# First batch of an attention-and-FFN kernel: one load, two fillers, one quad's division and its banks moved

## The chip, the cores and the metric

The kernel runs on one core of a Trainium2 chip. The core has a matrix engine (TensorE, in the profile PE, its weight loads PEld), a vector engine (VectorE, DVE), an activation engine (ScalarE, ACT), GpSimd (POOL) and a sync engine (SP) that only issues DMAs; POOL and ACT issue DMAs too. Matrix results land in PSUM, eight banks of 512 float32 columns on 128 partitions. The metric is the device time of one execution in microseconds (us), the median of several runs.

## The reference: attention with beacon keys, then a max-out FFN

For each of 8 batches and 8 heads there are 576 queries, 576 keys and values and 16 "beacon" keys and values, all of width 64, in float32. The beacons stand in front of the keys and are never masked; the rest is causal.

```python
k_all = np.concatenate([beacon_k, k], axis=2)
v_all = np.concatenate([beacon_v, v], axis=2)
scores = scale * np.matmul(q, k_all.transpose(0, 1, 3, 2))
scores = np.where(causal, -1000000000.0, scores)
a = np.exp(scores - scores.max(-1, keepdims=True))
a /= a.sum(-1, keepdims=True) + 1e-09
attn = np.matmul(a, v_all)                                  # (8, 8, 576, 64)
x = attn.transpose(0, 2, 1, 3).reshape(4608, 512)
h = np.maximum(np.maximum(x @ w1, x @ w2), x @ w3)          # 512 -> 768, three times
out = h @ w_out                                             # 768 -> 512
```

## The kernel before, in words

**Tiling.** Heads go in pairs (four pairs a batch, 32 in all), pairs in quads (two quads a batch). A pair's queries and keys are transposed on PE into `qT` and `kT` (128 partitions: two heads of width 64). Scores stand with keys on partitions and queries on columns, cut into four groups of columns a pair (`groups_0` in batch 0, 464, 288, 496 and 416 columns a head); `emit_scores(p, gi)`, here `S_`, makes a group in two banks, one for each head, and ACT writes its exponential into `at_sb` in bfloat16. `M` (`emit_masks`) clears what is above the diagonal, on DVE in batch 0 where its third argument says so, else on POOL. `P` (`pv_rest`) multiplies by values: part 0 uses ones in place of values and so makes the sums, parts 1 and 2 use even and odd value columns. Its first 64 query columns (`HEAD`) are made apart by `pv_heads`. A quad is divided by its sums: ACT takes Ln and then Exp with scale -1 (`invert_rest`), DVE takes a reciprocal for the heads (`invert_heads`), and DVE multiplies into `xT`, bfloat16 (`multiply_heads`, `multiply_rest`). The FFN reads `xT`: `mm1` units (three matrices with a running maximum into `hT`), then `mm2` units to the output. The first units of the FFN work on 256 tokens at a time (`mm1_halves`), two row blocks in one bank.

**Order.** It is written out by hand, one list for all engines, and every engine takes its own instructions strictly in that order. An instruction waits until what it reads is there and until earlier readers of what it overwrites are done; for PSUM this goes by whole banks. `start` loads halves of pairs 0 and 1 (SP and ACT issue), quads with a cast by POOL (`load_quad`), a mask triangle `tri` and an identity made by POOL, and keeps PE busy with matmuls whose result nobody reads (`keep_busy(n)`, 320 columns, bank 5). `first_batch` interleaves transposes `T`, scores, masks, value casts `V` (POOL) and value products. From pair 4 on, `emit_burst(p)` makes all four groups of a pair, one for each pair of banks, `emit_pv_whole(quad, order)` a whole quad, and FFN units fill PE in between.

**Banks.** In batch 0, `sc_psum` alternates banks 0-1 and 2-3 for the score groups. Quad 0 has bank 4 for its sums, 5 and 6 for the parts and 7 for the heads; quad 1 takes its banks from `sc_psum` when the last score group has been read: 2 sums, 3 heads, 0 and 1 parts. From batch 1 on, `free_banks` is a list in the order of use; `next_bank` takes the first and puts it last, `next_pairs` orders whole pairs by when they were used. `emit_burst(8)` takes the bank pairs 0-1, 2-3, 4-5, 6-7 for groups 0 to 3, and right after it `emit_pv_whole(3)` takes 0 for the sums, 1 and 2 for the parts, 3 for the heads. Its raw parts are copied out by ACT first (line 682), then the heads (683), then Ln is taken of the sums (688).

Of the kernel before, what the change touches and what calls it, by code (L numbers as in the profile page):

```python
# [10 lines left out]
BF16 = mybir.dt.bfloat16  # L11
AF = mybir.ActivationFunctionType
# [5 lines left out]
def kernel(  # L18
# [13 lines left out]
    nc = tc.nc  # L32

    B, H, S, D = q.shape
# [200 lines left out]
    def load_half(p, i, queue):  # L235
        st = half_pool.tile([QP, 2, HR, D], FP32, name=f"h32{i}")
        queue.dma_start(
            out=st.rearrange("p h r d -> p h (r d)"),
            in_=half_source(p // PPQ, 0, i, 2 * (p % PPQ), 2),
        )  # L240
        stage["half", p, i] = st
# [219 lines left out]
    def keep_busy(n, cols=320, ffn=False):  # L461
        ps = ffn_psum.tile() if ffn else pv_bank(1)
        for _ in range(n):
            nc.tensor.matmul(  # L464
                ps[:, 0:cols], busy[:, 0:128], busy[:, 0:cols], start=True, stop=True
            )
# [111 lines left out]
    recips = {}  # L578
    ready = [-1]

    def open_pv(quad, sums, parts, heads):
        pv_tiles[quad] = (sums, parts[:, 0], parts[:, 1], heads, parts)
        recips[quad] = nrm_pool.tile([128, S], FP32, name="recip")

    def pv_matmuls(quad, part, out, t, q0, q1, start, stop):
# [32 lines left out]
    def invert_heads(quad):  # L618
        nc.vector.reciprocal(recips[quad][:, 0:HEAD], pv_tiles[quad][3][:, 0:HEAD])

    def invert_rest(quad, q0, q1):
        recip = recips[quad][:, q0:q1]
        sums = pv_tiles[quad][0][:, q0 - HEAD : q1 - HEAD]
        nc.scalar.activation(out=recip, in_=sums, func=AF.Ln)
        nc.scalar.activation(out=recip, in_=recip, func=AF.Exp, scale=-1.0)

    def multiply_heads(quad):
        b, g = divmod(quad, n_quad)
# [4 lines left out]
            recips[quad][:, None, 0:HEAD].to_broadcast([128, 2, HEAD]),  # L633
        )

    def multiply_rest(quad, q0, q1, i0=0, i1=2):
        b, g = divmod(quad, n_quad)
        c0 = b % RING * S
        nc.vector.tensor_mul(
            xT[:, 2 * g + i0 : 2 * g + i1, c0 + q0 : c0 + q1],  # L640
            pv_tiles[quad][4][:, i0:i1, q0 - HEAD : q1 - HEAD],
            recips[quad][:, None, q0:q1].to_broadcast([128, i1 - i0, q1 - q0]),
        )

    def emit_pv_whole(quad, order=(0, 1, 2, 3), split=False):
        b, g = divmod(quad, n_quad)
# [58 lines left out]
    hTs = {}  # L705
# [178 lines left out]

    def start():
        keep_busy(8, 480)
        load_half(0, 0, nc.sync)
        load_half(0, 1, nc.scalar)
        load_beacons(0, 1, bk32_0)
        load_half(1, 1, nc.scalar)  # L890
        load_half(1, 0, nc.sync)
        make_identity(nc, ident)
        nc.gpsimd.memset(tri, 1.0)
        nc.gpsimd.affine_select(
            out=tri,
            in_=tri,
            compare_op=ALU.is_ge,
            fill=0.0,
            base=0,
            pattern=[[1, 128]],  # L900
            channel_multiplier=-1,
        )
        load_quad(1, 0)
        load_quad(0, 1)
        load_quad(1, 1)
        cast_half(0, 0, by_dve)
        cast_half(0, 1, by_act)
        by_dve(bk16_0, bk32_0)
        turn_part(0, 0, 0, 6, by_act)
        turn_part(0, 0, 1, 7)  # L910
        keep_busy(2)
        turn_beacons(0, 1, bk16_0)
        cast_half(1, 1, by_dve)
        cast_half(1, 0, by_dve)
        keep_busy(1)
        emit_scores(0, 0)
        turn_part(1, 0, 1, 5)
        turn_part(1, 0, 0, 4)
# [3 lines left out]
    def F(n=1, new_ps=ffn_psum.tile, close=False):  # L922
        for _ in range(n):
            assert emit_ffn(END, new_ps, close)

    def F_in(bank, copy):
        drain[0] = copy
        F(1, partial(acc.__getitem__, (slice(None), bank)))

    def first_batch():  # L930
        T(2, 0, 0, 6, by_act)
        T(3, 0, 0, 7)
        load_v(0, 0, nc.vector)
        load_v(0, 1)
        load_beacons(1, B_PE, bk32_1)
        S_(1, 0)
        T(2, 0, 1, 5)
        T(3, 0, 1, 4)
        S_(2, 0)
        T(0, 1, 0, 6)  # L940
        T(0, 1, 1, 7)
        S_(3, 0)
        T(1, 1, 0, 5)
        T(1, 1, 1, 4)
        M(0, 0, True)
        S_(0, 1)
        fill(6)
        S_(0, 2)
        T(2, 1, 0, 6)
        T(3, 1, 0, 4)  # L950
        M(1, 0, True)
        S_(1, 1)
        T(2, 1, 1, 7)
        T(3, 1, 1, 5)
        S_(1, 2)
        S_(0, 3)
        for p in range(PPB):
            M(p, 1)
        M(0, 2, True)
        M(1, 2, True)  # L960
        V(0)
        load_w(0, [0])
        V(1)
        load_w(0, [1])
        V(2)
        load_cast(PPB)
        load_w(1, [0])
        V(3)
        load_w(1, [1])
        V(4)  # L970
        load_cast(PPB + 1)
        load_cast(PPB + 2)
        load_w(2)
        load_cast(PPB + 3)
        open_pv(0, acc[:, 4], acc[:, 5:7], acc[:, 7])
        P(0, (0,), (0, 1))
        pv_heads(0)
        S_(1, 3)
        M(0, 3, True)
        M(1, 3, True)  # L980
        S_(2, 1)
        P(0, (0,), (), (1, 3))
        S_(2, 2)
        M(2, 0, True)
        M(3, 0, True)
        P(0, (0,), (), (2, 4))
        S_(3, 1)
        M(2, 2, True)
        invert_heads(0)
        multiply_heads(0)  # L990
        P(0, (1, 2), (0, 1))
        S_(3, 2)
        S_(2, 3)
        M(3, 2, True)
        P(0, (1, 2), (), (1, 2))
        S_(3, 3)
        M(2, 3, True)
        M(3, 3, True)
        P(0, (1, 2), (), (3,))
        first = sc_psum.tile()  # L1000
        open_pv(1, first[:, 0], sc_psum.tile(), first[:, 1])
        P(1, (0,), (0, 1))
        pv_heads(1)
        P(1, (0,), (), (1, 3))
        P(0, (1, 2), (), (4,))
        P(1, (0,), (), (2, 4))
        for quad in range(n_quad):
            invert_rest(quad, HEAD, HALF)
        invert_heads(1)
        multiply_rest(0, HEAD, HALF)  # L1010
        multiply_heads(1)
        for part in (1, 2):
            P(1, (part,), (0, 1), (1, 2, 3, 4))
            multiply_rest(1, HEAD, HALF, part - 1, part)
        ready[0] = 0
        for quad in range(n_quad):
            invert_rest(quad, HALF, S)
            multiply_rest(quad, HALF, S)
        by_act(bk16_1, bk32_1)
        ready[0] = 1  # L1020
        F_in(7, by_act)
        F_in(3, by_dve)
        F_in(4, by_act)
        turn_beacons(1, B_PE, bk16_1)
        place_beacons(PPB, by_act)
        F_in(5, by_dve)
        F_in(6, by_act)
        free_banks[:] = [0, 1, 2, 7, 3, 4, 5, 6]
        turn_pair(PPB, by_act)
        load_v(1, 0, nc.vector)  # L1030
        load_v(1, 1)
        drain[0] = by_dve
        F(1, last_pair(), True)
# [47 lines left out]
    def emit_all():  # L1081
        start()
        first_batch()
        pending = second_batch()
        n_y = 0
        v_tiles.pop(0)

        for p in range(2 * PPB, NPAIR):
            b, pi = divmod(p, PPB)
            emit_burst(p)  # L1090
            if p == 2 * PPB:
                pending()
            finish = emit_pv_whole(p // 2 - 1) if p % 2 == 0 else None
            for gi in range(NG):
                emit_masks(p, gi)
            allowed = max((b - 1) * UPB + (-2, 4, 10, 16)[pi], done[0] + 2)
            n = 0
            while may_emit(allowed):
                n_y = len(y_out)
                close = not may_emit(allowed, 1)  # L1100
                emit_ffn(allowed, last_pair() if close else next_psum, close)
                store_y(n_y)
                n += 1
                if n == 1 and p + 1 < B_PE * PPB:
                    turn_pair(p + 1, by_act)
                    place_beacons(p + 1, by_act)
                if n == 2:
                    for fn in plan.pop((p, 0), ()):
                        fn()
            assert n >= 2  # L1110
            if finish:
                finish()
            for s in range(2):
                for fn in plan.pop((p, s), ()):
                    fn()
            if pi == 0:
                v_tiles.pop(b - 1)
        assert not plan and not loads
        finish = emit_pv_whole(NPAIR // 2 - 1)
        for _ in range(4):  # L1120
            emit_ffn(END, next_psum)
        finish()
        store_y(len(y_out))
        while emit_ffn(END - 1, next_psum):
            store_y(len(y_out))
        mm2_last(n_tokb - 1, TOKB // 128 - 1, (0, 320, 512))
# [33 lines left out]
```

## Time and profile before

| | |
|---|---|
| time, median of 3 runs | 283.64 us (282.99 to 285.45) |
| the profiled execution | 283.08 us, of which 281.4 us from first to last instruction |
| granted TensorE clock over the span | 0.998 |
| PE busy | 273.4 us (97%) |
| DVE, ACT, POOL busy | 171.1, 162.8, 131.5 us |
| chain that ended last | PE 92%, ACT 5%, DVE 1% |

All durations in this document are from one profiled execution, the time from several. In a line of the timeline the columns are start and length in us, engine, source line, operation, what is written and read with its shape, the number of instructions merged into the line, and in brackets the engine's idle time before it and what ended it. Lines that merge several instructions give the time that they cover together. PE's ends are modelled: consecutive matmuls overlap in the rows, so their cost is read from start to start. The granted clock stands as 1.00 also where the record has nothing.

### The profile page before, as it was taken

The numbers are of one execution on the slowest core, as the hardware profiler recorded it, in microseconds if no ns is written. First come the engines' busy times: TensorE is split into PE (matmuls) and PEld (weight loads), VectorE is DVE, ScalarE is ACT, GpSimd is POOL, SyncE is SP. The second block draws the span as 40 slices with busy tenths as digits, with TensorE's granted clock in tenths as the row PEclk, the third lists the DMA queues.
The fourth block names the chain that finished last, engine by engine and source line by source line (L and its number), as shares of the span: only waits on it lengthen the run. The fifth ranks groups of instructions, "written<-read, shape, count | busy, mean of one in ns | idle before, by whom it ended". The sixth has DMA issues, their size and how long they took to land.

```text
span 281.4 us, 7592 instructions
## 1 busy us (share of the span) xinstructions
PE 273.4 (97%) x2994; PEld 156.1 (55%) x2994; DVE 171.1 (61%) x299; ACT 162.8 (58%) x307; POOL 131.5 (47%) x273
## 2 busy tenths in 40 slices
PE   7889999999999999999999999999999999999994
PEld 3547765556565555555556886555555554444442
DVE  3877565574837476464737383638363847876772
ACT  3896897968668566756675758585858540000000
POOL 7185378557286945484548655673254200000000
PEclk9999999999999999999999999999999999999999
DMA  8999999999997899999999999989672003004004
GB/s 132 209 200 209 213 171 150 210 247 304 258 210 220 230 242 214 204 223 275 219 199 235 236 249 214 228 229 206 115 142 93 2 2 149 0 1 151 0 0 149
DMA packets 85316, 48.83 MB, mean 174 GB/s; under 512 B 64417, under 2 KB 80033, under 8 KB 85281
## 3 DMA queue, kind: packets, MB, share of 16 engines
q1 hardware_dynamic: 78320, 42.25, 67.3%
q0 software_dynamic: 6544, 5.80, 13.4%
q8 instruction: 23, 0.38, 0.6%
q10 hardware_dynamic: 416, 0.30, 0.4%
q14 instruction: 13, 0.10, 0.1%
HBM read 35.13 MB, written 14.22 MB: 175 GB/s over the span
## 4 chain that ended last, share of the span: by engine, by line
PE 92%; ACT 5%; DVE 1%; issue 0%
PE acc L721 47%; PE acc L774 16%; PE acc L672 10%; PE acc L520 8%; PE acc L751 4%; ACT at_sb L514 3%; PE acc L404 2%; PE acc L464 2%; PE acc L591 1%; ACT at_sb L540 1%; PE acc L505 1%; PE acc L792 0%; PE acc L423 0%; ACT recip L688 0%; ACT raw L682 0%
## 5 line engine op out<-in xcount | busy, mean ns | idle before, releaser
L721 PE MATMUL acc<-xT,w_sb 128*128 128x512 bf16 (+4 forms) x752 | 135.7, 336 | 0.0
L738 DVE TENSOR_TENSOR hT<-hT,acc 128x512 bf16<-128x512 bf16 (+1 forms) x104 | 70.1, 677 | 61.5 <-PE acc L721 54.8
L721 PEld LDWEIGHTS <-w_sb 128*128 128x128 bf16 x752 | 69.7, 98 | 59.3
L564 POOL TENSOR_SCALAR_AFFINE_SELECT at_sb<-at_sb 128x256 bf16<-128x256 bf16 x168 | 60.0, 377 | 82.0 <-ACT at_sb L540 81.9
L540 ACT ACTIVATE at_sb<-acc 128x208 bf16<-128x208 f32 (+3 forms) x140 | 89.6, 737 | 4.9 <-PE acc L520 3.3
L774 PE MATMUL acc<-w_out_sb,hT 128*128 128x512 bf16 (+2 forms) x246 | 48.4, 348 | 0.4 <-ACT recip L688 0.4
L740 ACT CAST hT<-acc 128x352 bf16<-128x352 f32 x18 | 8.1, 452 | 47.0 <-PE acc L721 47.0
L774 PEld LDWEIGHTS <-hT 128*128 128x128 bf16 x246 | 22.7, 98 | 22.1 <-DVE hT L738 1.6
L275 POOL CAST p<-st 96x768 bf16<-96x768 f32 x44 | 34.9, 822 | 0.0
L781 DVE COPY y<-acc 128x512 f32<-128x512 f32 (+1 forms) x35 | 21.9, 628 | 20.9 <-PE acc L774 14.0
L740 DVE CAST hT<-acc 128x512 bf16<-128x512 f32 (+1 forms) x48 | 26.6, 554 | 9.8 <-PE acc L721 9.5
L799 ACT COPY y<-acc 128x320 f32<-128x320 f32 x1 | 0.4, 425 | 46.0 <-PE acc L792 46.0
L520 PE MATMUL acc<-qT,kT 64*128 64x208 bf16 (+1 forms) x336 | 26.1, 279 | 0.0
L672 PE MATMUL acc<-at_sb,v_sb 128*32 128x336 bf16 (+5 forms) x672 | 22.8, 281 | 0.0
L699 DVE TENSOR_TENSOR xT<-raw,recip 128x576 bf16<-128x576 f32 x28 | 21.1, 795 | 0.9 <-ACT recip L547 0.9
L520 PEld LDWEIGHTS <-kT 64*128 64x128 bf16 x336 | 15.4, 93 | 11.1 <-issue 0.7
L320 POOL CAST v_sb<-st 128x1536 bf16<-128x1536 f32 (+2 forms) x21 | 18.3, 894 | 0.0
L672 PEld LDWEIGHTS <-v_sb 128*32 128x32 bf16 (+1 forms) x672 | 14.5, 96 | 6.5
L682 ACT COPY raw<-acc 128x512 f32<-128x512 f32 x28 | 15.7, 637 | 2.8 <-PE acc L672 2.7
L672 PE MATMUL acc<-at_sb,ones 128*32 128x512 bf16 (+3 forms) x336 | 15.0, 284 | 0.0
L514 ACT ACTIVATE at_sb<-acc 128x928 bf16<-128x928 f32 (+3 forms) x16 | 12.6, 865 | 1.7 <-PE acc L505 1.7
L751 PE MATMUL acc<-xT,w_sb 128*128 128x256 bf16 x96 | 11.9, 273 | 0.0
(76 smaller groups left out, 174.6 us busy)
## 6 DMA issues: line engine op xcount, KB each, us to landing
out_dram<-y SPq DMA_DIRECT2D x35, 256.0 KB, 3.9
st<-in_q_dram SPq DMA_DIRECT2D x22, 288.0 KB, 4.5
st<-in_k_dram SPq DMA_DIRECT2D x22, 288.0 KB, 4.9
st<-in_v_dram SPq DMA_DIRECT2D x24, 256.0 KB, 6.3
w_sb<-in_moe_w_dram POOLq DMA_DIRECT2D x6, 384.0 KB, 7.7
q_dram<-p SPq DMA_DIRECT2D x16, 144.0 KB, 2.5
k_dram<-p SPq DMA_DIRECT2D x16, 144.0 KB, 2.4
st<-in_v_dram SPq DMA_DIRECT2D x8, 224.0 KB, 5.4
```

The source lines that it names most:

```text
L275: cast(t16.rearrange("p r h d -> p h r d"), st[0:QP, i * NQ2 : (i + 1) * NQ2].rearrange("p (h r d) -> p h r d", h=2, r=QR),)
L520: nc.tensor.matmul(ps, kTs[p % NT][hs, 128 * t : 128 * t + 128], qTs[p % NT][hs, q0:q1], start=True, stop=True, tile_position=(64 * e, 0),)
L540: nc.scalar.activation(out=both_heads(p, gi)[:, e0:e1], in_=acc[:, first + e0 : first + e1, 0 : g_width(p, gi)], func=AF.Exp, scale=scale,)
L564: nc.gpsimd.affine_select(out=view, in_=view, compare_op=ALU.is_ge, fill=0.0, base=x0, pattern=[[0, 2], [1, hi - lo]], channel_multiplier=-1,)
L672: nc.tensor.matmul(acc[32 * j : 32 * j + 32, bank, lo + q0 - qa : lo + qb - qa], lhsT, at_view(PPQ * quad + j // 2, t, j % 2, q0, qb), sta ...
L699: nc.vector.tensor_mul(xT[:, 2 * g + i, c0 : c0 + S], raw[:, i], recip)
L721: nc.tensor.matmul(ps[:, a:b], w_in[i][:, ct, 128 * ft : 128 * (ft + 1)], xT[:, ct, x0 : x0 + b - a], start=(ct == 0), stop=(ct == n_ct - 1),)
L738: nc.vector.tensor_max(h[:, lo:hi], h[:, lo:hi], ps[:, lo:hi])
L740: (by_act if hi < TOKB else by_dve)(h[:, lo:hi], ps[:, lo:hi])
L751: nc.tensor.matmul(ps, w_in[i][:, ct, 128 * (ft + f) : 128 * (ft + f + 1)], xT[:, ct, tb * TOKB + lo : tb * TOKB + hi], start=(ct == 0), s ...
L774: nc.tensor.matmul(ps[:, lo:hi], hT[:, ft, 128 * tt : 128 * (tt + 1)], w_out_sb[:, ft, lo:hi], start=(ft == 0), stop=(ft == n_ft - 1),)
L781: (by_act if hi < d_model else by_dve)(y[:, lo:hi], ps[:, lo:hi])
```

## The change

In batch 0: pair 1's first half of queries is loaded by POOL as its first instruction (before: by SP, third); `tri` is made after the six quad loads of POOL (before: ahead of them); `keep_busy(2)` ahead of the beacon keys' transposes goes. Quad 0's parts are multiplied earlier, its Ln and Exp are taken on all 512 columns at once, each between two exponentials, and its multiplication of columns 64 to 288 comes ahead of the last mask. Quad 1 is opened in banks 4 (sums), 7 and 3 (parts) and 2 (heads), so its sums and first part begin before the last score group. The first FFN unit (`first_unit`) runs in banks 0 and 1 and takes both row blocks' quad 0 channels ahead of quad 1's. `multiply_rest` is one instruction for each part. The list of free banks after batch 0 starts otherwise; with it the bank pairs 0-1 and 2-3 change places from pair 4 on. At pair 8, `emit_pv_whole` takes its four banks in the order (2, 0, 1, 3): the third for the sums, the first and second for the parts.

```diff
-    def open_pv(quad, sums, parts, heads):
-        pv_tiles[quad] = (sums, parts[:, 0], parts[:, 1], heads, parts)
+    def open_pv(quad, sums, p1, p2, heads):
+        pv_tiles[quad] = [acc[:, i] for i in (sums, p1, p2, heads)]
...
+    def take_log(quad, q0, q1):
+        sums = pv_tiles[quad][0][:, q0 - HEAD : q1 - HEAD]
+        nc.scalar.activation(out=recips[quad][:, q0:q1], in_=sums, func=AF.Ln)
+
+    def take_exp(quad, q0, q1):
+        recip = recips[quad][:, q0:q1]
+        nc.scalar.activation(out=recip, in_=recip, func=AF.Exp, scale=-1.0)
+
     def invert_rest(quad, q0, q1):
...
+        take_log(quad, q0, q1)
+        take_exp(quad, q0, q1)
...
-    def multiply_rest(quad, q0, q1, i0=0, i1=2):
+    def multiply_rest(quad, q0, q1):
...
+        for i in range(2):
+            nc.vector.tensor_mul(
+                xT[:, 2 * g + i, c0 + q0 : c0 + q1],
+                pv_tiles[quad][1 + i][:, q0 - HEAD : q1 - HEAD],
+                recips[quad][:, q0:q1],
+            )
...
     def start():
         keep_busy(8, 480)
+        load_half(1, 0, nc.gpsimd)
         load_half(0, 0, nc.sync)
         load_half(0, 1, nc.scalar)
         load_beacons(0, 1, bk32_0)
         load_half(1, 1, nc.scalar)
-        load_half(1, 0, nc.sync)
         make_identity(nc, ident)
+        load_quad(1, 0)
+        load_quad(0, 1)
+        load_quad(1, 1)
         nc.gpsimd.memset(tri, 1.0)
...
-        load_quad(1, 0)
-        load_quad(0, 1)
-        load_quad(1, 1)
         cast_half(0, 0, by_dve)
...
         turn_part(0, 0, 1, 7)
-        keep_busy(2)
         turn_beacons(0, 1, bk16_0)
...
+    def first_unit():
...
+        for g in range(n_quad):
+            for f in range(2):
+                for ct in (2 * g, 2 * g + 1):
+                    nc.tensor.matmul(
+                        acc[:, f, 0 : hi - lo],
+                        w_in[i][:, ct, 128 * (ft + f) : 128 * (ft + f + 1)],
+                        xT[:, ct, lo:hi],
+                        start=(ct == 0),
+                        stop=(ct == n_ct - 1),
+                    )
+        by_act(hTs[tb][:, ft : ft + 2, lo:hi], acc[:, 0:2, 0 : hi - lo])
...
-        open_pv(0, acc[:, 4], acc[:, 5:7], acc[:, 7])
+        open_pv(0, 4, 5, 6, 7)
         P(0, (0,), (0, 1))
         pv_heads(0)
         S_(1, 3)
         M(0, 3, True)
         M(1, 3, True)
+        P(0, (1, 2), (0,))
         S_(2, 1)
         P(0, (0,), (), (1, 3))
         S_(2, 2)
         M(2, 0, True)
         M(3, 0, True)
+        P(0, (1, 2), (1,))
+        S_(3, 1)
         P(0, (0,), (), (2, 4))
-        S_(3, 1)
-        M(2, 2, True)
+        take_log(0, HEAD, S)
         invert_heads(0)
         multiply_heads(0)
-        P(0, (1, 2), (0, 1))
+        M(2, 2, True)
+        P(0, (1, 2), (), (1,))
         S_(3, 2)
+        take_exp(0, HEAD, S)
+        P(0, (1, 2), (), (2,))
         S_(2, 3)
+        open_pv(1, 4, 7, 3, 2)
+        P(1, (0,), (0, 1))
+        P(0, (1, 2), (), (3,))
+        P(1, (1,), (0, 1))
         M(3, 2, True)
-        P(0, (1, 2), (), (1, 2))
         S_(3, 3)
         M(2, 3, True)
+        P(1, (0, 1), (), (1, 3))
+        P(0, (1, 2), (), (4,))
+        multiply_rest(0, HEAD, HALF)
         M(3, 3, True)
-        P(0, (1, 2), (), (3,))
-        first = sc_psum.tile()
-        open_pv(1, first[:, 0], sc_psum.tile(), first[:, 1])
-        P(1, (0,), (0, 1))
         pv_heads(1)
-        P(1, (0,), (), (1, 3))
-        P(0, (1, 2), (), (4,))
-        P(1, (0,), (), (2, 4))
-        for quad in range(n_quad):
-            invert_rest(quad, HEAD, HALF)
+        P(1, (2,), (0, 1), (1, 3))
+        P(1, (0, 1, 2), (), (2, 4))
+        invert_rest(1, HEAD, HALF)
+        invert_rest(1, HALF, S)
+        by_act(bk16_1, bk32_1)
         invert_heads(1)
-        multiply_rest(0, HEAD, HALF)
         multiply_heads(1)
-        for part in (1, 2):
-            P(1, (part,), (0, 1), (1, 2, 3, 4))
-            multiply_rest(1, HEAD, HALF, part - 1, part)
-        ready[0] = 0
-        for quad in range(n_quad):
-            invert_rest(quad, HALF, S)
-            multiply_rest(quad, HALF, S)
-        by_act(bk16_1, bk32_1)
+        multiply_rest(1, HEAD, HALF)
+        multiply_rest(0, HALF, S)
+        multiply_rest(1, HALF, S)
         ready[0] = 1
-        F_in(7, by_act)
-        F_in(3, by_dve)
-        F_in(4, by_act)
+        first_unit()
+        F_in(2, by_dve)
+        F_in(5, by_act)
         turn_beacons(1, B_PE, bk16_1)
         place_beacons(PPB, by_act)
-        F_in(5, by_dve)
-        F_in(6, by_act)
-        free_banks[:] = [0, 1, 2, 7, 3, 4, 5, 6]
+        F_in(6, by_dve)
+        F_in(4, by_act)
+        free_banks[:] = [7, 3, 0, 1, 5, 2, 6, 4]
...
-            finish = emit_pv_whole(p // 2 - 1) if p % 2 == 0 else None
+            finish = emit_pv_whole(p // 2 - 1, (2, 0, 1, 3) if p == 2 * PPB else (0, 1, 2, 3)) if p % 2 == 0 else None
```

More of the change, by code (lines that the diff above doesn't have):

```diff
@@ L619, in invert_heads @@
         nc.vector.reciprocal(recips[quad][:, 0:HEAD], pv_tiles[quad][3][:, 0:HEAD])
+    def take_log(quad, q0, q1):
[4 more added lines that the diff above has]
+        nc.scalar.activation(out=recip, in_=recip, func=AF.Exp, scale=-1.0)
     def invert_rest(quad, q0, q1):
[L622 to L625, printed above, removed]
+        take_log(quad, q0, q1)
+        take_exp(quad, q0, q1)
     def multiply_heads(quad):
@@ L634, in multiply_heads @@
         )
-    def multiply_rest(quad, q0, q1, i0=0, i1=2):
+    def multiply_rest(quad, q0, q1):
         b, g = divmod(quad, n_quad)
         c0 = b % RING * S
[L639 to L643, printed above, removed]
+        for i in range(2):
[4 more added lines that the diff above has]
+            )
     def emit_pv_whole(quad, order=(0, 1, 2, 3), split=False):
@@ L924, in F @@
             assert emit_ffn(END, new_ps, close)
+    def first_unit():
+        _, fn, (tb, ft, i, lo, hi) = units[done[0]]
+        assert done[0] == 0 and fn == mm1_halves
+        done[0] += 1
+        hTs[tb] = ffn_h.tile([128, n_ft, TOKB], BF16, name="hT")
+        for g in range(n_quad):
[9 more added lines that the diff above has]
+        by_act(hTs[tb][:, ft : ft + 2, lo:hi], acc[:, 0:2, 0 : hi - lo])
     def F_in(bank, copy):
```

## The prediction

> **What bounds the kernel.** I read the stretches first, then PE's waits, then the chain. The first fence has two answers: busy time by stretch (length, then busy us and count of PE, PEld, DVE, ACT, POOL, then clock, DMA share, GB/s), and PE's waits between 23.7 and 270 us.
>
> ```profile
> 9.95:21.05 11.10, 9.63 (x207) 5.58 (x206) 8.94 (x29) 10.77 (x15) 7.20 (x13) 1.00 1.16 210
> 21.05:23.64 2.59, 2.45 (x72) 1.64 (x61) 2.39 (x8) 2.39 (x7) 2.13 (x4) 1.00 1.18 216
> 23.64:270.00 246.36, 245.93 (x2626) 141.37 (x2626) 149.86 (x236) 144.53 (x278) 116.89 (x243) 1.00 0.82 176
> ...
> PE acc L774 <- ACT recip L688: 0.4, 1, 0.4
> ```
>
> From 23.64 us, PE idles once, for 0.4 us. So only two things move the end: when PE's unbroken work begins, and what is done to that one idle. Before 23.64 the chain in order of time runs through ACT's exponentials:
>
> ```profile
> 9.95 6.25 ACT at_sb L514 x8
> ...
> 18.53 2.52 ACT at_sb L514 x3
> ...
> 21.42 1.75 PE acc L591 x52
> 23.17 0.02 issue
> 23.19 0.40 DVE xT L639
> ```
>
> From 9.95 to 21.05 ACT is busy 10.77 of 11.10 us. Then come the last mask, 52 value matmuls, a multiplication, the FFN.
>
> **Step 1: the start.** PE, DVE and the landings of the halves (`h`) and quads, with the scores of pairs 0 (6.44) and 1 (8.35):
>
> ```profile
> 5.19 0.73 PE L464 MATMUL acc<-busy 128*128 128x320 bf16 x2
> 5.86 0.27 PE L360 MATMUL acc<-ident,bk 16*128 16x16 bf16 x4
> 6.06 0.45 PE L464 MATMUL acc<-busy 128*128 128x320 bf16 x1
> 6.44 0.57 PE L505 MATMUL acc<-qT,kT 64*128 64x176 bf16 x4
> ...
> 8.35 0.37 PE L505 MATMUL acc<-qT,kT 64*128 64x176 bf16 x4 [0.40 <-DVE qT L431]
> ...
> 5.43 0.46 DVE L431 COPY kT<-acc 128x288 bf16<-128x288 bf16 x1 [0.31 <-PE acc L423]
> 5.81 0.41 DVE L245 CAST h<-h 96x384 bf16<-96x384 f32 x1
> 6.68 0.35 DVE L245 CAST h<-h 96x384 bf16<-96x384 f32 x1 [0.46 <-DMA h<-in_q_dram]
> ...
> DMA to landing us min/median/max: 3.1/3.5/4.9
> DMA to landing us min/median/max: 5.3/5.5/5.8
> ```
>
> Two of the three fillers ahead of the scores go; 5.86 minus 5.19 is 0.67 us. What is late next is the key copy on DVE, done at 5.89, so the scores of pair 0 start at about 5.95 for 6.44: 0.5 us won. Pair 1 wins it only if its query, issued by SP at 1.76 and landed 4.9 later, is there by 6.2, when DVE has cast the key half. Its new issue on POOL is at 0.81. What a half takes there no row shows: from below the fastest SP half (3.1, landing 3.9), from above the slowest quad (5.8, landing 6.6, nothing won). I take the fastest quad, 5.3: it was also the first transfer of its queue. That gives 6.1. The POOL issue takes 0.68 to 0.81 (its quad issues), and `tri` (1.32 to 1.88) moves behind the quads: these come 0.2 to 0.3 later, since 0.57 of 0.8 is given back. The second quad load was issued at 2.64 and at the median landed about 8.1; its transposes at 8.65 would now start at 8.2 and must wait to 8.4. `tri` itself is first read at 11.74. I take 0.35 us won at the exponential of 9.95; bounds 0.5 won and 0.1 lost (the extra load shares the queues with pair 0's halves).
>
> [...]
>
> **Step 2: Ln and Exp between exponentials.** Two instructions of 512 columns come into ACT's full queue. The nearest rows are L688 (Ln, 512) with 0.69 and L547 (Exp, 576) with 0.69; from start to start 0.49 (54.66 to 55.15) and 0.58 (50.41 to 50.99). I take 0.55 each, 1.1 together. Of it 0.34 lies in ACT's one idle, ahead of 18.53: there it waited for scores that stood behind 16 value matmuls, which are now earlier. The last exponential ends at 21.05 - 0.35 + 1.1 - 0.34 = 21.45. All else behind them (masks, bank 4's new owner) has slack: quad 1's sums need bank 4 after Ln at about 18.3, and the PE queue behind them, the last scores, is not needed by ACT until 20.6.
>
> **Step 3: the tail.** DVE now has quad 0's multiplication (two of 0.39, 0.1 overlapped) ahead of the last mask: from the mask of group (2,3), done at about 21.05, to 21.7. So the mask starts 0.2 late, at 21.65, and its second instruction ends at 22.1 (0.44 for both). Then PE has only the late sums before ACT can go on: sums done 22.35 (0.21 for an 80-column matmul), Ln 0.37 to 22.74, Exp 0.39 to 23.15, two multiplications to 23.86. PE meanwhile does 16 other matmuls and the FFN unit's first five; three are left (0.11 each, by the starts of unit 1's rows), and the second unit starts at 24.23. Before, five were left at 23.64: 24.18. So +0.05: what moved out of the tail (0.8 of Ln and Exp, 28 matmuls) was bought with ACT's 1.1. The beacon transposes now want bank 2, copied out by DVE behind four multiplications of 288 columns (0.45 each, between 0.39 for 224 and 0.56 for 448): DVE is through at about 26.0, PE there at 25.97, another +0.05.
>
> **Step 4: pair 8.** ACT and PE:
>
> ```profile
> 50.41 0.69 ACT L547 ACTIVATE recip<-recip 128x576 f32<-128x576 f32 x1
> 50.99 0.95 ACT L540 ACTIVATE at_sb<-acc 128x928 bf16<-128x928 f32 x1
> ...
> 50.60 0.86 PE L672 MATMUL acc<-at_sb,ones 128*32 128x512 bf16 x20
> ...
> 55.40 0.91 PE L774 MATMUL acc<-w_out_sb,hT 128*128 128x352 bf16 x5 [0.41 <-ACT recip L688]
> ```
>
> The sums (`ones`) start first, at 50.60, in the first bank, read by the exponential of group 0. In the new order they take the third bank, which group 1's exponential (50.99, 0.95 long) frees at 51.94. PE takes its matmuls in order, so all 72 wait: 51.98 - 50.60 = 1.38 us lost. The idle before 55.40 goes, as the FFN unit then finds banks of the raw copies, read out by 54.67: PE would have started at 54.91 (its weight load stood ready), 0.49 won. ACT's copies begin at 53.56 anyway, 0.2 after the first part is done; the second is ready at about 54.2 for 54.03. Net +0.9, and PE has no later idle that could take it up.
>
> Sum: 0.05 + 0.05 + 0.9 = **+1.0 us**. On the profiled execution (281.4 of span, 1.7 around it) 283.08 becomes 284.1; the median of the runs stood 0.56 above it, so **284.6**.
>
> **Rivals.**
> A. *The query lands no earlier than 6.66*, or the quads are 0.5 later: the change does not do what it says. For it: POOL's 5.3 to 5.8. Nothing of the 0.35 is won: 285.0. Chance 0.17.
> B. *Pair 8 does not stall*, if the sums' bank is free at 50.6. For it: in the old order a part waited for the same exponential only to 51.94, hardly at all. Against: the sums are first in the queue. Then 284.6 - 1.4 = 283.2. Chance 0.12.
> C. *The tail wins more*: the query lands at once, and Ln and Exp cost 0.45 each: -0.4, 284.2; with B 282.8. Chance 0.07.
> D. *Slower: the fillers carried the clock.* Four score matmuls took 0.57 us at 6.44 and 0.37 at 8.35, so PE changed speed in between (the trace's record of the granted clock begins at 7.42, at full speed); the eight first fillers, 480 columns each, start 0.40 apart, at half the rate of later matmuls. If the lost fillers put the change off by one such stretch (1.53 to some 7.4 holds less than two, so about 3.4 us, to 10.8), two score groups at 0.2 and two sets of transposes at 0.2 (0.64 against 0.45) cost 0.8: 285.4. If PE is still slow past 10.8, at most its busy 2.94 us up to 14.24 doubles, less 0.47 of idle: +2.5 more, 287.9. That is the point from which it decides. Chance 0.09 for one stretch, 0.04 for more. [...]
>
> The forecast itself, 283.9 to 285.3, has 0.51. The range from 283.0 to 286.0 holds it, A, C, most of B and one stretch of D. One per cent, about what a measurement of this kernel can tell from no change, is 2.8 us: 0.02 for faster (B and C with more on top), 0.93 for the same, 0.05 for slower (D).
>
> **What would show it.** The scores of pair 0 near 5.95 and the third exponential near 9.6 (step 1); the last exponential's end at about 21.4 (2); the second FFN unit near 24.2 (3); a PE idle of about 1.3 us ahead of the sums after pair 8's scores, ended by ACT's exponential, and no idle ended by L688 (4). Wrong would make it a PE clock that rises after 8 us, a query cast after 6.7, or a start of PE's unbroken work off by over 0.5 us.

## The result and the profile after

| | before | after |
|---|---|---|
| time, median of 9 runs each | 282.99 us (282.15 to 285.45) | 286.0 us (285.16 to 286.53) |
| the profiled execution | 283.08 us, span 281.4 | 286.47 us, span 284.8 |
| granted TensorE clock over the span | 0.998 | 0.982 |
| PE busy | 273.4 us (97%) | 274.0 us (96%) |
| second FFN unit of batch 0 starts | 24.18 | 27.04 |
| scores of pairs 8 and 9 start | 49.60, 56.80 | 52.47, 60.56 |

The ratio after to before is 1.01, with a 95% interval of 1.007 to 1.013: slower by 3.0 us, where +1.0 us was forecast. 284.6 stood on the three runs shown (283.64); on these nine it would have been 284.0. The time lies at the very end of the range (286.0), in the part of it that was kept for rival D. Of the 3.4 us by which the profiled span is longer, 2.86 stand at the second FFN unit, 0.89 more come between the scores of pairs 8 and 9, and 0.39 is given back behind PE's last matmul, which ends at 277.77 before and 281.54 after.

In the edited kernel the lines are numbered otherwise: 672 is now 679, 688 is 695, 721 is 728, 774 is 781, 639 is 646, Ln 624 and Exp 625 are 623 and 627; `first_unit` is 940.

The page of the kernel after: the span, PE's row, the granted clock in 40 slices of 7.1 us (tenths of full speed), and the chain's shares.

```profile
span 284.8 us, 7559 instructions
...
PE 274.0 (96%) x2962; PEld 156.0 (55%) x2992; DVE 171.2 (60%) x302; ACT 163.4 (57%) x305; POOL 133.4 (47%) x274
...
PEclk9669999999999999999999999999999999999999
...
PE 89%; ACT 4%; DMA 2%; issue 2%; DVE 1%; POOL 1%; POOLq 0%
```

The second and third slices of the clock read 6; before, all 40 read 9. The page's busy shares say nothing of it: PE is 96% busy, for 97%.

The stretches of the kernel after that answer to those of before (exponentials, tail, unbroken work), then PE alone in the stretches at whose ends the trace's record of the granted clock changes. Columns: length, busy us and count of each engine, clock, DMA share, GB/s.

```profile
9.47:24.20 14.73, 13.48 (x238) 6.74 (x240) 9.20 (x30) 12.28 (x16) 9.92 (x17) 0.68 1.12 199
24.20:27.10 2.90, 2.13 (x37) 1.27 (x31) 2.54 (x10) 1.87 (x5) 0.65 (x1) 1.00 1.13 204
27.10:273.40 246.30, 243.40 (x2593) 140.68 (x2620) 149.17 (x237) 144.06 (x276) 116.69 (x241) 1.00 0.80 174
...
5.24:8.65 3.41, 2.63 (x45) 1.00 1.36 151
8.65:18.89 10.24, 9.14 (x116) 0.50 1.14 197
18.89:24.20 5.31, 4.95 (x128) 1.00 1.11 196
```

The stretch of the exponentials took 14.73 us, for 11.10 before, and in it ACT is no longer full (12.28 of 14.73; before 10.77 of 11.10). The clock came up at 5.24, stayed for 3.41 us, and then was half for 10.24 us, three times 3.41. What that does to ACT is seen in the chain of the kernel after in order of time (start, length, what):

```profile
4.72 5.46 DMA quad<-in_k_dram
...
10.23 0.45 PE acc L423 x6
10.68 0.52 PE acc L505 x4
11.20 0.02 issue
11.22 0.95 ACT at_sb L514
12.17 0.45 issue
12.62 0.60 PE acc L505 x4
...
15.39 2.53 ACT at_sb L514 x3
...
20.80 0.49 ACT recip L623
21.28 0.89 ACT at_sb L514
22.18 0.51 ACT recip L627
22.69 0.76 ACT at_sb L514
```

Between 10 and 15 us the chain goes through PE's transposes (`L423`) and scores (`L505`), where before it went through ACT alone. The set of four score matmuls at 12.62 (64x288) takes 0.60 us; at full clock, in the kernel before, such a set takes 0.39. ACT waited for scores for 3.8 us in all, for 1.7 before. The chain also runs through a late quad, landed at 10.19, which held PE for 0.42 us.

The start and pair 8 of the kernel after, on PE:

```profile
5.32 0.25 PE L360 MATMUL acc<-ident,bk 16*128 16x16 bf16 x4
5.50 0.31 PE L464 MATMUL acc<-busy 128*128 128x320 bf16 x1
5.93 0.37 PE L505 MATMUL acc<-qT,kT 64*128 64x176 bf16 x4
...
7.68 0.37 PE L505 MATMUL acc<-qT,kT 64*128 64x176 bf16 x4 [0.35 <-ACT qT L431]
...
52.47 1.07 PE L520 MATMUL acc<-qT,kT 64*128 64x208 bf16 x12
54.85 0.87 PE L679 MATMUL acc<-at_sb,ones 128*32 128x512 bf16 x20 [1.31 <-ACT at_sb L540]
```

Pair 0's scores are at 5.93 (predicted 5.95), and the wait at pair 8 is there (1.31, predicted 1.38). What the forecast had not in its sum is what lies between 8.65 and 18.89.

### The profile page after: what moved, and what is told of

It reads as the page before. It is cut to its first block, busy times and chain, and to the rows that moved or that the text cites. A ratio compares the mean times of both kernels' runs of the same rounds, so it can differ in the third digit from the quotient of the medians.

```text
span 284.8 us, 7559 instructions
## 1 busy us (share of the span) xinstructions
PE 274.0 (96%) x2962; PEld 156.0 (55%) x2992; DVE 171.2 (60%) x302; ACT 163.4 (57%) x305; POOL 133.4 (47%) x274
## 3 DMA queue, kind: packets, MB, share of 16 engines
q0 software_dynamic: 6592, 5.95, 13.5%
## 4 chain that ended last, share of the span: by engine, by line
PE 89%; ACT 4%; DMA 2%; issue 2%; DVE 1%; POOL 1%; POOLq 0%
PE acc L728 46%; PE acc L781 16%; PE acc L679 11%; PE acc L520 8%; PE acc L758 4%; PE acc L404 2%; ACT at_sb L514 2%; DMA quad<-in_k_dram 2%; DVE at_sb L562 1%; PE acc L505 1%; POOL quad L266 1%; PE acc L423 1%; PE acc L799 0%; ACT at_sb L540 0%; DVE xT L646 0%
## 5 line engine op out<-in xcount | busy, mean ns | idle before, releaser
L728 PE MATMUL acc<-xT,w_sb 128*128 128x512 bf16 (+4 forms) x728 | 134.2, 335 | 1.4 <-issue 0.2
L564 POOL TENSOR_SCALAR_AFFINE_SELECT at_sb<-at_sb 128x256 bf16<-128x256 bf16 x168 | 60.9, 384 | 84.5 <-ACT at_sb L540 83.8
L514 ACT ACTIVATE at_sb<-acc 128x928 bf16<-128x928 f32 (+3 forms) x16 | 13.4, 868 | 3.8 <-PE acc L505 3.8
L679 PEld LDWEIGHTS <-ones 128*32 128x32 bf16 (+1 forms) x336 | 7.8, 96 | 5.6 <-issue 1.3
```

The source lines that it names most:

```text
L514: nc.scalar.activation(out=both_heads(p, gi), in_=ps[:, :, 0 : g_width(p, gi)], func=AF.Exp, scale=scale)
L564: nc.gpsimd.affine_select(out=view, in_=view, compare_op=ALU.is_ge, fill=0.0, base=x0, pattern=[[0, 2], [1, hi - lo]], channel_multiplier=-1,)
L679: nc.tensor.matmul(acc[32 * j : 32 * j + 32, bank, lo + q0 - qa : lo + qb - qa], lhsT, at_view(PPQ * quad + j // 2, t, j % 2, q0, qb), sta ...
L728: nc.tensor.matmul(ps[:, a:b], w_in[i][:, ct, 128 * ft : 128 * (ft + 1)], xT[:, ct, x0 : x0 + b - a], start=(ct == 0), stop=(ct == n_ct - 1),)
```

## The experiments

Three questions: is it the clock and not the new list that costs the 2.86 us; which part of the new start brings the clock down; and is the wait at pair 8 an addition of its own? The theory after the result: the steps of the forecast hold, +1.0 us, and about 2 us are the granted clock, rival D. The rival theories: the new list costs more than was worked out, or the late quads do.

All kernels of a set ran on one chip beside 24 to 31 runs of the kernel before, whose medians there were 282.88, 282.75 and 282.83 us. The times of a kernel fall into two groups, so for each the number of executions below 283.5 us is given. Of the 86 runs of the kernel before, 64 lie below it, with a median of 282.7, and most of the others at 283.9 to 284.4 with a mean granted clock of 0.985 to 0.988: 0.012 of a span of 282 us is 3.4 us of clock, or 6.8 us at half clock. So the kernel before has the same trouble in a quarter of its executions. Where pair 8 has its new order, 0.9 us is added to the bound.

| kernel | start | fillers added | median us (range), 10 runs | below the bound | ratio to before, 95% |
|---|---|---|---|---|---|
| the change | new | | 286.0 (285.16 to 286.53), 9 runs | 0 of 9 | 1.007 to 1.013 |
| a_order: its pair 8 as before | new | | 285.16 (284.2 to 286.03) | 0 | 1.003 to 1.009 |
| b_start: before, new start | new | | 284.89 (283.99 to 285.46) | 0 | 1.002 to 1.008 |
| a_batch: new list alone | old | | 282.9 (282.5 to 283.42) | 10 | 0.994 to 1.001 |
| a_fill: the change | new | two old | 285.44 (283.7 to 287.01) | 3 | 1.002 to 1.010 |
| b_nofill: before | old, without its two | | 285.37 (282.41 to 286.16) | 2 | 1.001 to 1.008 |
| b_loads: before | old, new loads | | 283.19 (282.43 to 284.88) | 5 | 0.998 to 1.004 |
| a_pad: as a_order | new | three | 283.04 (282.67 to 285.67) | 7 | 0.997 to 1.004 |
| a_busy: as a_order | new | two old, three | 283.16 (282.62 to 285.34) | 7 | 0.997 to 1.005 |
| a_own: the change | new | two old, three | 284.07 (283.58 to 288.22) | 8 | 1.002 to 1.008 |
| b_order1: before, other order | old | | 283.02 (282.26 to 285.67) | 6 | 0.997 to 1.004 |
| b_busy: as b_order1 | old | two | 282.62 (282.38 to 283.26) | 10 | 0.997 to 1.001 |

### Pair 8 with its old order

```diff
-            finish = emit_pv_whole(p // 2 - 1, (2, 0, 1, 3) if p == 2 * PPB else (0, 1, 2, 3)) if p % 2 == 0 else None
+            finish = emit_pv_whole(p // 2 - 1) if p % 2 == 0 else None
```

> The changed kernel, with the old bank order at pair 8. All theories of the start agree here; this tests step 4 alone. If step 4 holds, the 1.31 us idle ahead of the sums at 54.85 goes, the 0.41 us idle ended by L695 (Ln of the sums) comes back, and the time falls by 0.9 us, from 286.0 to 285.1. If the stall is taken up elsewhere (rival B), the time stays at 286.0 or rises by 0.4.

285.16 us, 0.84 under the change (0.73, if each is taken against the runs of the kernel before beside it). PE's waits after batch 0 (engine, line, what it waited for, total, times, longest), with their line of `a_order`, then with that of the kernel after:

```profile
PE acc L781 <- ACT recip L695: 0.4, 1, 0.4
```

```profile
PE acc L679 <- ACT at_sb L540: 1.3, 1, 1.3
```

Both waits are as step 4 has them, one for the other. From the scores of pair 8 to those of pair 9 it is 7.19 us in this run (52.11, 59.30), 8.09 in the kernel after, 7.20 before. The order costs 0.9 us by itself, wherever the start ends.

### The new start alone, and the new list alone

`b_start` is the kernel before with `start` of the change; `a_batch` the change with `start` of before and the old order at pair 8.

```diff
     def start():
         keep_busy(8, 480)
+        load_half(1, 0, nc.gpsimd)
...
         load_half(1, 1, nc.scalar)
-        load_half(1, 0, nc.sync)
         make_identity(nc, ident)
+        load_quad(1, 0)
+        load_quad(0, 1)
+        load_quad(1, 1)
         nc.gpsimd.memset(tri, 1.0)
...
-        load_quad(1, 0)
-        load_quad(0, 1)
-        load_quad(1, 1)
...
-        keep_busy(2)
```

> The kernel before with the new start alone (query by GpSimd, quads and triangle reordered, two fillers gone). Clock theory: without the fillers the granted clock is half for some stretches between 8 and 19 us, as in the changed kernel's profile (8.65 to 18.89); PE's unbroken work begins 2 to 3 us later, time 285 to 286. Landing theory: the second keys of quad 0 land at 10.2 for 9.5 us, the exponential of pair 3 starts 0.4 later, and nothing more: 283.4. Reorder theory (the loss comes from the new list of batch 0): 282.6, the 0.35 us of step 1 won.

> The changed kernel with the old start and the old bank order at pair 8, so the new list of batch 0 and its banks alone. Clock and landing theories: the clock rises at about 7.4 us and stays, the second FFN unit starts 0.3 to 0.5 us later than in the kernel before (steps 2 and 3 without the start's gain), time 283.4. Reorder theory: 285, with the clock full throughout.

The new list costs some 0.25 us (282.9, against 282.65 for the undisturbed runs of the kernel before beside it, 282.88 for all), half of what the expectation had; the new start costs 2.0 us, 284.89 where the clock theory said 285 to 286. PE in `b_start`:

```profile
5.90:9.31 3.41, 2.62 (x49) 1.00 1.34 140
9.31:16.14 6.83, 6.20 (x90) 0.50 1.29 213
```

The same picture as in the kernel after, with two stretches at half clock. 2.0 for the start and 0.9 for pair 8 make 2.9 of the change's 3.0 us.

`a_batch` also shows steps 2 and 3 at full clock. ACT there:

```profile
9.90 8.25 ACT L514 ACTIVATE at_sb<-acc 128x928 bf16<-128x928 f32 x11 [0.24 <-PE acc L505]
...
18.04 0.60 ACT L623 ACTIVATE recip<-acc 128x512 f32<-128x512 f32 x1
18.52 1.02 ACT L514 ACTIVATE at_sb<-acc 128x992 bf16<-128x992 f32 x1
19.40 0.65 ACT L627 ACTIVATE recip<-recip 128x512 f32<-128x512 f32 x1
19.92 1.64 ACT L514 ACTIVATE at_sb<-acc 128x832 bf16<-128x832 f32 x2
```

From start to start Ln costs 0.48 and Exp 0.52. The last exponential ends at 21.56, the second unit starts at 24.40: 0.22 later than before.

### The two fillers put back, and taken from the kernel before

`a_fill` is the change with these two, `b_nofill` the kernel before without them:

```diff
         turn_part(0, 0, 1, 7)
+        keep_busy(2)
         turn_beacons(0, 1, bk16_0)
```

> The changed kernel with keep_busy(2) put back at its old place, everything else as changed. Clock theory: the granted clock stays full after its first rise, and 2 us or more come back: 284 or less. Landing theory: the landings are as before the fillers, the time stays at 286.0. Reorder theory: 286.0 to 286.4.

> The kernel before without the two fillers ahead of the beacon keys; its loads stay. Theory 'fillers': they alone kept the clock up; without them it falls to half for two or three stretches of 3.41 us, as in the run of the new start: 284.3 to 285.3, the third exponential near 9.5 and the last one's end near 22.3. Theory 'loads': PE is short of work because the quads land late and the fillers matter little: full clock from about 7.4 on in most executions, 282.5 to 283.2, the last exponential's end at 21.0 or 0.3 before it.

Taking the two fillers from the kernel before costs 2.6 us at the median and moves 8 of 10 executions above the bound: they are a cause by themselves, without any change of loads. Putting them back into the change mends 3 of 10; these three, 283.70 to 283.86, are 1.1 above the undisturbed runs of the kernel before: the forecast's +1.0. The median stays at 285.44, so the fillers are not all; it lies between the clock theory's 284 or less and the 286.0 of the others, and bears out none of them.

The profiled execution of `b_nofill` shows a second form of the trouble. Its record begins only at 17.18, at full clock; what the trace has no record of counts as 1.00 in the clock column, so the clock is read from the length of the scores' rows:

```profile
5.65 0.27 PE L360 MATMUL acc<-ident,bk 16*128 16x16 bf16 x4 [0.22 <-DVE bk L908]
...
6.23 0.57 PE L505 MATMUL acc<-qT,kT 64*128 64x176 bf16 x4
...
8.14 0.57 PE L505 MATMUL acc<-qT,kT 64*128 64x176 bf16 x4
...
9.65 0.57 PE L505 MATMUL acc<-qT,kT 64*128 64x176 bf16 x4 [0.31 <-DVE kT L431]
```

0.57 us for four score matmuls, three times over, as in the change while its record says half clock (0.57 at 8.86 and 10.61; 0.37 at 5.93 and 7.68, at full clock): PE was at half clock there. The profiled execution took 285.49 us.

### The loads alone

`b_loads` has `b_start`'s edit but for its last line, which stays:

```diff
+        load_half(1, 0, nc.gpsimd)
...
         turn_part(0, 0, 1, 7)
         keep_busy(2)
```

> The kernel before with pair 1's query loaded by GpSimd and the quads issued ahead of the triangle, the two fillers kept. Theory 'fillers': the clock stays up and the time is 282.5 to 283.2. Theory 'loads': PE waits for the late quads between 6.5 and 10, the clock falls to half behind it in most executions, and the time is 284 to 285, as with the whole new start (284.89). Were both needed, each alone would be within 0.5 of the kernel before.

283.19 us, interval around 1. Half of the executions are below the bound, for 24 of 31 of the kernel before beside them: too few to tell a small harm from none. Neither theory's number came true. The loads are at most a small part.

### More fillers behind the first transposes

`a_pad` is `a_order` with the three lines below, `a_busy` has `keep_busy(2)` as well, and `a_own` is `a_busy` with the change's own order at pair 8.

```diff
+        fill(0, 448)
         S_(1, 0)
         T(2, 0, 1, 5)
         T(3, 0, 1, 4)
+        fill(2, 448)
         S_(2, 0)
         T(0, 1, 0, 6)
+        fill(0, 448)
         T(0, 1, 1, 7)
```

> The changed kernel with the default order at pair 8 and the three fillers of 448 columns, without the two fillers ahead of the beacon keys. Theory 'an unbroken stretch': the clock rises only after 3.41 us in which PE hardly idles; the short idles of 0.1 to 0.4 between 5.2 and 6.6 break it, so that some executions rise early and are then held by the three later fillers (near 283) and others rise only at 15 to 20 us (285 to 286): a median of 284.5 to 285.5, wide apart. Theory 'work between 7 and 10 us': only the stretch after the rise matters, the three fillers hold it, 282.6 to 283.3 in nearly all executions.

> The changed kernel with the default order at pair 8, the two fillers back, and three fillers of 448 columns more: ahead of the scores of group (1,0), ahead of those of (2,0), and between the two query transposes of the second quads. Each takes 0.19 us at full clock. Theory 'clock': what the change lost is the granted clock, and PE kept busy between 6 and 10 us gets it back: full clock in nearly all executions and 282.6 to 283.2, against 285.16 for the changed kernel with that order alone. Theory 'order of the work': the loss is in the new list or in the late quads themselves, and the fillers only add to it: 285.2 to 285.8.

> The whole change, its own order at pair 8 included, with the two fillers back and the same three fillers of 448 columns between 7.8 and 9.5 us that held the clock in the run with the default order (283.16 there). Theory 'clock and order, added': what is left over the kernel before is the idle ahead of the sums at pair 8, 0.84 to 0.9: 283.9 to 284.2, the idle 1.3 again and the distance between the eighth and ninth burst of transposes 8.1. Theory 'one hides the other' (the idle at pair 8 costs less once the start is fast): 283.2 to 283.5.

The three matmuls, whose results nobody reads, bring `a_order` from 285.16 to 283.04, to the level of the kernel before, and with the two old ones as well it is 283.16. So the theory that work between 7 and 10 us decides gave `a_pad`'s median; but three of ten stay disturbed, and its profiled execution (285.56) is of the other theory's form: the record of full clock begins at 17.38 only. Up to there PE is busy without a gap:

```profile
3.73:7.14 3.41, 3.41 (x28) 1.00 1.33 173
7.14:17.38 10.24, 10.24 (x126) 1.00 1.20 187
17.38:24.20 6.82, 6.46 (x156) 1.00 1.09 194
```

Up to 17.38 there is no record, so 1.00 tells nothing there; a set of scores takes 0.57 us at 5.95, 8.15 and 9.76, its length in the change at half clock (8.86, 10.61). PE is busy for 10.24 of 10.24 us there, and at 9.76 the scores were still at half clock: in this execution busy time alone did not bring full clock by then.

`a_own` is the forecast with its cover restored: 284.07, eight of ten at 283.58 to 284.33. Their median, 283.89, is 1.2 above that of the 18 undisturbed runs of the kernel before beside it (282.71), fillers included, and 0.9 above the seven of `a_busy` (283.0). Pair 8's wait is unchanged, 1.3 us, so clock and order add up.

```profile
7.03:10.44 3.41, 3.09 (x51) 1.00 1.35 160
...
52.61 0.86 PE L679 MATMUL acc<-at_sb,ones 128*32 128x512 bf16 x20 [1.31 <-ACT at_sb L540]
```

### When the clock rises, in all profiled executions

One execution each; the boundaries are from the record of the granted clock, PE's busy time and its count of matmuls from the stretches. For `b_nofill` and `a_pad`, whose record begins late, the stretches are 17.18 to 23.43 and 17.38 to 24.20.

| kernel | full clock from | busy in the 3.41 us behind the rise | and then |
|---|---|---|---|
| a_order | 4.53 | 2.40, 38 matmuls | half for 10.24 us |
| the change | 5.24 | 2.63, 45 | half for 10.24 us |
| a_fill | 5.84 | 2.49, 48 | half for 10.24 us |
| b_start | 5.90 | 2.62, 49 | half for 6.83 us |
| b_order1 | 6.02 | 2.51, 49 | half for 6.82 us |
| b_busy | 4.79 | 3.32, 53 | full |
| a_own | 7.03 | 3.09, 51 | full |
| a_busy | 7.27 | 3.09, 53 | full |
| b_loads | 6.81 | 2.49, 58 | full |
| a_batch | 7.07 | 2.50, 58 | full |
| before | 7.42 | 2.58, 63 | full |
| b_nofill | 17.18 | 4.94 of 6.25, 114 | full |
| a_pad | 17.38 | 6.46 of 6.82, 156 | full |

In the five executions whose clock fell, the fall comes 3.41 us behind the rise (3.42 in `b_order1`) and the next rise 6.82 to 10.24 us behind the fall, two or three times as much; the first rise comes at another time in each. `b_order1` has the start of the kernel before, unaltered, and fell when its rise came at 6.02; before itself, risen at 7.42, held. In these executions the old start, with the old loads or the new, rises at about 7 (6.81 to 7.42) and stays, or rises at 6.02 and falls; with two fillers more (`b_busy`) it rises at 4.79 and stays. In `b_nofill` and `a_pad`, both without the two old fillers, no change is on record before 17.18 and 17.38.

Busy time doesn't tell the stretches that fell (2.40 to 2.63) from those that held (2.49 and more). The count of matmuls does for the eleven that rose early, 38 to 49 against 51 to 63, but that is one execution each, and no run changes the count alone. Where fillers of 448 columns lie in the stretch behind an early rise, it is busy for 3.09 to 3.32 us, and all three held (`b_busy`, `a_own`, `a_busy`); the old start without them held with 2.49 to 2.58 in three executions and fell with 2.51 in `b_order1`, and 22 of 86 runs of the kernel before are disturbed.

In none of the stretches behind which the clock fell was PE idle for long: in the change it was busy for 2.63 of 3.41 us and idle for at most 0.43 at a time (0.53 in `a_order`), and in `a_pad` the scores were still at 0.57 us at 8.15 and 9.76 with no idle from 7.14 on. What of PE's work the clock follows is not shown; nor is what transposes do for it, since no run here had them apart from other work.

### Another order at pair 8, and a candidate

`b_order1` is the kernel before with this; `b_busy` has the first two of the three fillers above besides.

```diff
-            finish = emit_pv_whole(p // 2 - 1) if p % 2 == 0 else None
+            finish = emit_pv_whole(p // 2 - 1, (1, 0, 2, 3) if p == 2 * PPB else (0, 1, 2, 3)) if p % 2 == 0 else None
```

> The kernel before with the order sums to the second bank, first part to the first, at pair 8. The second bank is read last by the copy of raw values that ends near 50.5, so the sums start at 50.6 as before; the first part takes the bank that group 0's exponential frees at about 50.9, and the unit behind them finds a free bank: the idle of 0.41 ended by Ln goes and nothing comes in its place, 282.4 against 282.9. If the order costs by itself (step 4's other end: what matters is which exponential the first 20 matmuls wait for), PE waits 0.4 to 1.3 ahead of the sums: 282.9 to 283.8.

> The kernel before with two fillers of 448 columns more, ahead of the scores of groups (1,0) and (2,0), and at pair 8 the sums in the second bank and the first part in the first. Theory 'clock': its own disturbed executions (8 of 31) go, since the first stretch at full clock is denser; 282.4 to 282.9 in nearly all of them, the median 0.1 to 0.4 under the kernel before's. Theory 'fillers only cost': each delays the transposes by 0.2, 283.0 to 283.3.

`b_order1` won nothing (283.02, interval around 1), for a reason that neither side had: the idle of 0.41 us went, and the next one came.

```profile
55.72 1.48 PE L774 MATMUL acc<-w_out_sb,hT 128*128 128x352 bf16 x12
57.56 0.89 PE L520 MATMUL acc<-qT,kT 64*128 64x208 bf16 x12 [0.36 <-ACT qT L438]
```

The scores of pair 9 now wait 0.36 us for their query copy on ACT; from pair 8's scores to pair 9's it is 7.15 us, for 7.20. ACT's rows from 51.22 to the end of that copy at 57.51 leave no idle, so its work behind pair 8 is the limit there.

`b_busy` had all ten executions between 282.38 and 283.26, seven of them below the 282.9 that the clock theory named as the upper end; the median is 282.62 against 282.83, the ratio 0.9988 with an interval of 0.997 to 1.001. It is not shown to beat the kernel before; what it shows is a smaller spread (the kernel before beside it reached 284.41). Its profiled execution rose early, at 4.79, and held:

```profile
4.79:8.20 3.41, 3.32 (x53) 1.00 1.43 165
8.20:11.61 3.41, 3.11 (x60) 1.00 1.43 221
```

## Why the prediction was right and wrong

**Step 1, the start: right in itself, and it decided the other way.** The third exponential starts at 9.47, 0.48 before its old time, for 0.35 predicted. The query landed at 5.58, not 6.1: 4.2 us after its issue, below the 5.3 that I had taken from the quads. The issue itself was later than predicted, 1.39 for 0.81; the profile shows nothing that POOL waited for between 0.71 and 1.39, and in the kernel before its first instruction, no DMA, starts at 0.81. The quads came otherwise than "0.2 to 0.3 later": the first two 1.0 earlier (6.12, 6.89 for 7.12, 7.95), the last four 0.2 to 0.85 later. One of these, landed at 10.19, held PE for 0.42 us, and so may be part of the 2.86. It was no cause of the clock's fall, which is at 8.65.

**Step 2, Ln and Exp: right.** 1.1 us were put in for the two, 0.34 taken up; at full clock `a_batch` shows 1.00 put in and, from the third exponential to the end of the last, 0.57 lost (11.66 against 11.09) for 0.76.

**Step 3, the tail: right.** From the last exponential's end to the second FFN unit it is 2.84 us in the kernel after and in `a_batch`, 3.14 before; predicted 2.78.

**Step 4, pair 8: right.** 0.9 predicted; 0.89 in the trace, 0.84 by the medians of the runs with and without. The forecast's reading that all 72 matmuls wait behind the sums held, and rival B (no stall) is out.

**Rival A** (the query lands no earlier) is out by 5.58; **rival C** (+0.6 in all) is not borne out by the executions of `a_fill` and `a_own` at full clock, 1.1 and 1.2 above those of the kernel before, fillers included. These have the two old fillers back, and with them not the whole of step 1's gain; no execution of the change itself held its clock. So the sum of +1.0 us is borne out by its parts, and for the change as a whole it isn't shown.

**Rival D happened, and the step that failed is that the forecast put the clock at nothing: it gave D a chance of 0.13, and none of nine runs escaped it.** D's price was 0.8 us for one stretch and up to 3.3 for more; measured is 2.0 (`b_start`), for two or three stretches. No row of the kernel before shows the stretch of about 3.4 us in that price; what the runs showed in its place is 3.41 us between rise and fall (5.24 to 8.65 in the change), and then 6.82 to 10.24 us at half clock. That 286.0 is still inside the range is luck, since the range was made for one stretch and the kernel lost more. Two things were wrong in D. I worked with a clock that rises late. In the profiled execution of the change it rises earlier than before, at 5.24, and then falls; the late rise is the other form, in `b_nofill` and `a_pad`. And I took the rise at 7.42 of one profiled execution for a property of the kernel. It is one draw: 22 of 86 runs of the kernel before went over the bound themselves, and the three runs shown with it, up to 285.45, gave a hint of that spread which I left unread. The sign that I named, a clock that rises after 8 us, is not what the profiled execution shows; the other one, a start of PE's unbroken work off by over 0.5 us, is (27.04 for 24.23).

What stays open: what of PE's work the clock follows (busy time alone does not tell, 2.40 to 2.63 us where it fell and 2.49 and more where it held), and why the loads landed otherwise.

## What to carry to other kernels

A filler that hides behind nothing and feeds nobody may hold the clock: before taking one away, look at the granted clock over several executions, not one (here 22 of 86 runs of the kernel before were disturbed, and 8 of 10 with its two fillers gone, `b_nofill`). The start here, made of transposes and small score matmuls, lost about 2 us though PE looks busy: in `b_start` it was busy for 6.20 of the 6.83 us at half clock. Two or three matmuls of 128 rows and 448 columns (0.36 us in their rows), put where PE mostly waits anyway, bought it back in 7 to 10 of 10 executions. A matmul group moved to another bank is to be checked for the last reader of that bank, and what is queued behind it in order, before the idle that goes is counted as won: here each idle that went left a next one (in `b_order1` 0.41 us went and 0.36 came).

## What the runs showed of the hardware

- In five executions PE's granted clock fell to half behind a stretch of 3.41 us in which PE was busy for 2.40 to 2.63 us (no idle in it longer than 0.53 in `a_order`, 0.43 in the change), and came back only after 6.82 to 10.24 us, though in `a_order` PE was busy 3.10, 2.95 and 3.41 of 3.41 us in them; in `a_pad` the scores at 8.15 and 9.76 were at half clock (0.57 us) with PE busy 10.24 of 10.24 from 7.14 on.
- Four score matmuls (64x176) took 0.37 us at full clock (5.93, 7.68) and 0.57 at half (8.86, 10.61) in the change; four of 64x288 took 0.39 at full clock in the kernel before (11.78) and 0.60 at half in the change (12.62).
- A plain load of a half issued by POOL as its first DMA landed 4.2 us after its issue, between SP's 3.2 and the 4.9 that pair 1's query took on SP before; and with it ahead of them, the first two quads took 3.4 and 3.5 us, for 5.3 before.
- In the last stretch, from PE's last matmul to the end, the same work took 3.60 us before and 3.21 after.
